# One core, attention and two feed-forward layers: the first batch's rows of values for local attention issued on ScalarE's DMA queue

## The chip, the core and the metric

The kernel runs on one core of a Trainium2 chip. Five engines work side by side, each with its own list of instructions that it takes strictly in order: PE (TensorE, matmuls and transposes on the tensor engine), DVE (VectorE), ACT (ScalarE), POOL (GpSimd) and SP (SyncE, which here only issues transfers). A transfer (DMA) is issued by an engine's instruction and then moved by 16 DMA engines. Engines wait for one another, and for transfers, through semaphores. The metric is the time of one execution on the device in microseconds (us); lower is better.

## The reference

Three layers follow one another. B = 4 batches, H = 8 heads, S = 576 positions, D = 64.

```python
# attention: a downsampled branch plus a local branch
q_d, k_d, v_d = means of q, k, v over groups of 4 positions
out_d = softmax(scale * q_d @ k_d^T) @ v_d          # repeated 4 times along S
scores = where(|i - j| < 4, scale * q @ k^T, -1e9)  # local: 7 diagonals
out_local = softmax(scores) @ v
x = (out_up + out_local) as [2304, 512]
# first feed-forward layer: [512 -> 2048 -> 512], ELU between
x = elu(x @ moe_w_in) @ moe_w_out
# second: gated, [512 -> 1536 -> 512]
out = (silu(x @ moe2_w_gate) * (x @ moe2_w_val)) @ moe2_w_out
```

The weights come as 64-bit floats and are unpacked into 32-bit ones on the chip.

## The kernel before

**Units.** Local attention of one batch is cut into six *units* of 96 positions. A unit loads its rows of q (192 KB), of k (224 KB) and of v (256 KB; four pieces of 32 rows, or five where a piece at the sequence's edge is split). In the code these are `load_rows`, called from `add_unit` and, for v, from the inner function `load_values`. PE transposes q and k (L495), ACT or DVE copies the transposed rows out of PSUM (L276 or L278, `qT` and `kT`), sums over groups of four go into `sums` (L506, L508, L509), PE computes the scores (L524), DVE masks them (L536) and takes maxima (L541), ACT takes exponentials (L548), the weights are transposed (L559) and spread (`bd`), and PE multiplies with v (L578); the result is copied to `f`.

**The downsampled branch.** When all six units' q and k are in `sums`, four pairs of heads follow (`add_pooled`): scores on PE (L619), maxima on DVE (L626), exponentials on ACT (L632, four per pair), normalizing on DVE (L638, L639, L642), transposes on PE (L660), products on PE (L673), copied into `xdT`. Their values are eight loads of 144 KB (L607).

**The feed-forward layers.** `x` is `f` plus `xdT` (L693). The work is cut into chunks of three units (288 positions). Chunk 0 of the first layer uses whole 32-bit products (L740 and L745, here called gemm1 and gemm2, 16 steps of 128 hidden columns each); later chunks split each number into two parts and make three products (L715 to L717). 32 weight tiles of 512 KB are loaded in the order in, out, in, out (L332, L337), 14 of them into places that are free from the start; ACT and DVE unpack them (L374, L377, L381, L383).

**Order.** All work is put into tasks by `add(engine, cost, due, fn, ...)`: each has an engine, an estimated cost and a due time, and a small event loop (`Work.run`) starts on each engine the ready task that is due first. The order that this gives is the order of each engine's instructions. The first batch's v rows were tasks of SP with cost 2.0 and a due time of their own (`v_due`), between q, k and the weights.

**Completion counters.** Every transfer signals its landing on one of eight counters, shown as DMAHW0 to DMAHW7 in the built program, which are handed out in turn. A transfer that takes a counter waits, on the engine that issues it, until the transfer that had the counter before has landed. When all transfers are issued by SP, each waits for the one eight places ahead of it.

Of the kernel before, what the change touches and what calls it, by code (L numbers as in the profile page):

```python
# [19 lines left out]
P = 128  # L20
R = 4
W = 2 * R - 1
QB = 32
# [7 lines left out]
UPC = 3  # L31
# [26 lines left out]
class Half(Buf):  # L58
# [5 lines left out]
    t = property(lambda self: False if self.whole.t is None else self.whole.t[:, self.i])  # L64
# [164 lines left out]
def attention_moe_moe(ctx: ExitStack, tc: tile.TileContext, q, k, v, w_in, w_out, w_gate, w_val, w_o2, ident_in, mask_in, band_in, picks_in, out):  # L229
    nc = tc.nc  # L230
    B, H, S, D = q.shape
# [40 lines left out]
    COPIER = "act", "dve"  # L272
# [13 lines left out]
    add = work.add  # L286
# [167 lines left out]

        return source[name][b, h0:h1].rearrange("h (u p r) d -> u p h (r d)", u=2, r=R)[u]

    def load_rows(name, b, first, count, t, p0=0):

        nc.sync.dma_start(  # L459
            out=t[p0:p0 + count].rearrange("p (h d) -> p h d", d=D),  # L460
            in_=source[name][b, :, first:first + count].rearrange("h t d -> t h d"))

    sums = {}

    def add_unit(n, due, load_due, rows=None, after=(), then=(), late=0.0, v_due=None, first=None):

        b, i = divmod(n, NU)
        q0 = i * U
        k0 = min(max(q0 - 8, 0), S - KU)
        off = PAD + q0 - k0  # L470
        tq, tk, tv = rows if rows else (qk_rows.new(), qk_rows.new(), v_rows.new())
        add("sp", 0.5, load_due, lambda: load_rows("q", b, q0, U, tq.t), writes=[tq], nbytes=U * H * D * 4 * 1.9, after=after)
        add("sp", 0.5, load_due + 0.1, lambda: load_rows("k", b, k0, KU, tk.t), writes=[tk], nbytes=KU * H * D * 4 * 1.9, after=after)

        def load_values():
            for s in range(NB):
                first = q0 + s * SB - (R - 1)
                lo, hi = max(first, 0), min(first + QB, S)
                p0 = s * QB + lo - first
                if hi - lo < QB:  # L480
                    nc.gpsimd.memset(tv.t[s * QB:(s + 1) * QB], 0.0)

                for a in range(lo, hi, QB // 2 if hi - lo < QB else QB):
                    load_rows("v", b, a, min(hi - a, QB // 2 if hi - lo < QB else QB), tv.t, p0 + a - lo)

        add("sp", 2.0, load_due + 4.0 if v_due is None else v_due, load_values, writes=[tv], nbytes=P * H * D * 4 * 3.1, after=after)
        if i == 0:
            sums[b] = sum_ring.new()
        qT, kT = place("qT"), place("kT")
        for which, t, dst, count, start, own in ((0, tq, qT, U, 0, 0), (1, tk, kT, KU, PAD, off)):  # L490
            pt = att_bank()

            def turn(t=t, count=count, pt=pt):
                for p in range(NP):
                    nc.tensor.transpose(pt.t[:, p * count:(p + 1) * count], t.t[:count, p * P:(p + 1) * P], ident[:count, :count])  # L495

            def keep(engine, dst=dst, count=count, start=start, pt=pt):
                copy(engine, dst.t[:, :, start:start + count], pt.t[:, :NP * count].rearrange("p (a t) -> p a t", a=NP))

            half = half_ring.new()  # L500

            def pool(engine, which=which, dst=dst, own=own, half=half):
                x = dst.t[:, :, own:own + U].rearrange("p a (g r) -> p a g r", r=R)
                to = sums[b].t[:, which, :, i * GU:(i + 1) * GU]
                if engine == "dve":
                    nc.vector.tensor_reduce(out=to, in_=x, op=ALU.add, axis=X)  # L506
                else:
                    nc.gpsimd.tensor_tensor(out=half.t, in0=x[:, :, :, :2], in1=x[:, :, :, 2:], op=ALU.add)  # L508
                    nc.gpsimd.tensor_tensor(out=to, in0=half.t[:, :, :, 0], in1=half.t[:, :, :, 1], op=ALU.add)  # L509

            begin = due if first is None else first
            add("pe", 0.4, begin - EAGER, turn, reads=[t], writes=[pt, dst], slack=SLACK, after=then)
            add(COPIER, (0.5, 0.55), begin + 1, keep, reads=[pt], writes=[dst], second=1)
            add(EITHER, (0.56, 1.1), begin + 2, pool, reads=[dst], writes=[sums[b], half])

        sc = [att_bank(), att_bank()]
        due += late

        def scores():
            for p in range(NP):  # L520
                for s in range(NB):
                    first = off + s * SB - (R - 1)
                    for j in range(2):
                        nc.tensor.matmul(  # L524
                            sc[j].t[s * QB:(s + 1) * QB, p * QB:(p + 1) * QB],
                            qT.t[j * D:(j + 1) * D, p, s * SB:s * SB + QB], kT.t[j * D:(j + 1) * D, p, first:first + QB],
                            start=True, stop=True)

        sm, st, pt, bd, pv = small["sm"].new(), small["st"].new(), small["pt"].new(), place("bd"), att_bank()

        add("pe", 0.8, due + 2 - EAGER, scores, reads=[qT, kT], writes=[*sc, sm], slack=SLACK)
        edge = 0 if i == 0 else 2 if i == NU - 1 else 1

        def masked():
            for j in range(2):
                nc.vector.tensor_tensor(  # L536
                    out=sm.t[:, j * NP:(j + 1) * NP], in0=sc[j].t[:, :NP * QB].rearrange("p (a k) -> p a k", a=NP),
                    in1=mask[:, edge:edge + 1].to_broadcast([P, NP, QB]), op=ALU.add)

        def maxima():  # L540
            nc.vector.reduce_max(out=st.t.rearrange("p h o -> p (h o)"), in_=sm.t, axis=X)  # L541

        def less(engine):
            two(engine).tensor_tensor(out=sm.t, in0=sm.t, in1=st.t.to_broadcast([P, H, QB]), op=ALU.subtract)

        def exps():
            x = sm.t.rearrange("p h k -> p (h k)")
            nc.scalar.activation(x, x, AF.Exp, scale=scale)  # L548

        def total():  # L550
            nc.vector.reduce_sum(out=st.t.rearrange("p h o -> p (h o)"), in_=sm.t, axis=X)
            nc.vector.tensor_scalar_add(st.t, st.t, 1e-9)
            nc.vector.reciprocal(out=st.t, in_=st.t)

        def weight(engine):
            two(engine).tensor_tensor(out=sm.t, in0=sm.t, in1=st.t.to_broadcast([P, H, QB]), op=ALU.mult)

        def turn_weights():
            nc.vector.transpose(out=pt.t.rearrange("p h k -> p (h k)"), in_=sm.t.rearrange("p h k -> p (h k)"))  # L559

        def spread(engine):
            for s in range(NB):
                rows = slice(s * QB, (s + 1) * QB)
                copy(engine, bd.t[rows, :, s * SB:(s + 1) * SB], pt.t[rows, :, :SB])

        add("dve", 0.56, due + 3, masked, reads=sc, writes=[sm])
        add("dve", 0.42, due + 3.1, maxima, reads=[sm], writes=[st])
        add(EITHER, (0.62, 0.65), due + 3.2, less, reads=[sm, st], writes=[sm])
        add("act", 0.4, due + 4, exps, reads=[sm], writes=[sm])
        add("dve", 0.8, due + 4.5, total, reads=[sm, st], writes=[st])  # L570
        add(EITHER, (0.5, 0.65), due + 5, weight, reads=[sm, st], writes=[sm])
        add("dve", 0.42, due + 5.5, turn_weights, reads=[sm], writes=[pt])
        add(("act", "dve"), (1.4, 1.5), due + 6, spread, reads=[pt], writes=[bd], second=1)

        def values():
            for p in range(NP):
                for j in range(2):
                    nc.tensor.matmul(  # L578
                        pv.t[j * D:(j + 1) * D, p * U:(p + 1) * U], tv.t[:, (2 * p + j) * D:(2 * p + j + 1) * D],
                        bd.t[:, j * NP + p], start=True, stop=True)  # L580

        xf = xf_ring.new()
        add("pe", 0.7, due + 7 - EAGER, values, reads=[tv, bd], writes=[pv, xf], slack=SLACK)
        add(COPIER, (0.5, 0.55), due + 8, lambda engine: copy(engine, xf.t, pv.t[:, :NP * U]), reads=[pv], writes=[xf], second=1)
        return xf
# [298 lines left out]
    with tc.manual_schedule():  # L884
# [9 lines left out]
        rows = [parts(2) for _ in range(NU)]  # L894
        vals = [x for _ in range(NU // 2) for x in parts(2)]
# [25 lines left out]

        xfs = {}
        for n in range(NU):
            xfs[n] = add_unit(n, 4.0 * n, -40 + 2 * n, rows=(*rows[n], vals[n]), late=0.0 if n < UPC else 24.0,
                v_due=-20.0 + n if n < UPC else 30.0 + n, first=0.5 * n - 8.0)
            if n == 0:
                load_mask()
        for p in range(NP):
# [6 lines left out]
        kept = {}  # L935
# [91 lines left out]
```

## Time and profile before

| | |
|---|---|
| median of 3 runs | 1028.29 us (1024.51 to 1029.45) |
| profiled execution | 1029.34 us, of which 1027.2 us span from first to last instruction |
| PE busy | 994.0 us, 97% of the span |
| DVE, ACT, POOL busy | 516.5, 414.5, 311.6 us |
| mean granted TensorE clock | 0.975 |
| moved by DMA | 91.19 MB |

Busy time is the time in which an engine executes. A wait shows as idle time in front of an instruction, with the name of what ended it. Because the engines take their lists in order, an instruction that waits holds back everything behind it on its engine.

### The profile page before, as it was taken

The page shows a single profiled execution, that of the slowest core. Times are in us where ns is not written, and L with a number is a line of the kernel's source. Part 1 is how long each engine was busy: PE and PEld are TensorE (multiplying, and loading weights), DVE is VectorE, ACT ScalarE, POOL GpSimd, SP SyncE. Part 2 cuts the span into 40 slices and gives each one's busy share as a digit, 9 for nine tenths or more (in the row PEclk, how much of TensorE's full clock was granted, in tenths as well). Part 3 has the DMA queues.
Part 4 walks back from the last instruction along what each step waited for, and adds up shares of the span by engine and source line. Part 5 has one row for each costly group of instructions (what it writes and reads, how often), then busy time and mean ns, then how long its engine had stood idle before and what let it go on. Part 6 is the DMA issues. An engine that isn't in the chain of part 4 may idle for free.

```text
span 1027.2 us, 19351 instructions
## 1 busy us (share of the span) xinstructions
PE 994.0 (97%) x7540; PEld 868.7 (85%) x7540; DVE 516.5 (50%) x1063; ACT 414.5 (40%) x1015; POOL 311.6 (30%) x358
## 2 busy tenths in 40 slices
PE   5899999899999999998999999999999999999998
PEld 4667789899998999998999888888888888888897
DVE  5888888876778767884124422232223222322232
ACT  4688865465554555545345421121112111211111
POOL 5230993652337333356259710010001000000000
PEclk8599999999999999999999999999999999999999
DMA  9799333654545654436024420020002000100000
GB/s 165 231 314 246 70 89 107 156 149 128 135 119 123 157 156 118 116 82 204 1 84 136 126 61 0 1 83 1 1 1 72 0 1 11 41 1 1 11 32 21
DMA packets 129003, 91.19 MB, mean 89 GB/s; under 512 B 73744, under 2 KB 116880, under 8 KB 128912
## 3 DMA queue, kind: packets, MB, share of 16 engines
q1 hardware_dynamic: 128768, 89.70, 32.4%
q8 instruction: 59, 0.97, 0.4%
q14 instruction: 32, 0.26, 0.1%
q10 hardware_dynamic: 144, 0.26, 0.1%
HBM read 71.06 MB, written 18.87 MB: 88 GB/s over the span
## 4 chain that ended last, share of the span: by engine, by line
PE 84%; DVE 7%; DMA 4%; SPq 2%; issue 2%; ACT 1%; POOL 0%; DVEq 0%; ACTq 0%; POOLq 0%
PE bank L715 25%; PE bank L716 24%; PE bank L717 24%; PE bank L740 2%; PE bank L745 2%; PE bank L578 1%; SPq L459 1%; DMA rows<-in_q_dram 1%; PE bank L524 1%; PE bank L495 1%; DVE mid L353 1%; PE bank L619 1%; DMA w<-in_moe_w_in_dram 1%; DVE f L693 1%; DMA w<-in_v_dram 1%
## 5 line engine op out<-in xcount | busy, mean ns | idle before, releaser
L715 PE MATMUL bank<-x,w 128*128 128x288 f32 (+2 forms) x928 | 318.0, 343 | 3.1 <-DVE e L788 2.6
L716 PE MATMUL bank<-x,w 128*128 128x288 f32 (+2 forms) x928 | 313.0, 337 | 0.0
L717 PE MATMUL bank<-x,w 128*128 128x288 f32 (+2 forms) x928 | 311.8, 336 | 0.0
L861 DVE TENSOR_TENSOR e<-bank,e 128x512 f32<-128x512 f32 (+1 forms) x120 | 76.3, 637 | 260.9 <-ACT e L858 179.3
L715 PEld LDWEIGHTS bank<-x,w 128*128 128x128 f32 x928 | 176.2, 190 | 25.0 <-DVE e L788 4.3
L716 PEld LDWEIGHTS bank<-x,w 128*128 128x128 f32 x928 | 176.7, 190 | 16.9 <-POOL x L703 0.3
L717 PEld LDWEIGHTS bank<-x,w 128*128 128x128 f32 x928 | 176.6, 190 | 16.8
L795 POOL TENSOR_TENSOR g<-e,g 128x288 fp32r<-128x288 f32 x112 | 94.9, 848 | 169.5 <-ACT g L276 124.9
L715 PE MATMUL bank<-g,w 128*128 128x288 f32 x448 | 135.2, 302 | 2.0 <-ACT o L276 2.0
L716 PE MATMUL bank<-g,w 128*128 128x288 f32 x448 | 132.3, 295 | 0.0
L717 PE MATMUL bank<-g,w 128*128 128x288 f32 x448 | 132.0, 295 | 0.0
L858 ACT ACTIVATE e<-bank 128x512 f32<-128x512 f32 (+1 forms) x60 | 33.2, 555 | 188.3 <-PE bank L717 188.3
L838 POOL TENSOR_TENSOR x<-x2r,x 128x512 fp32r<-128x512 f32 (+1 forms) x20 | 23.5, 1194 | 269.7 <-ACT x L837 269.7
L863 ACT CAST y<-e 128x512 fp32r<-128x512 f32 (+1 forms) x60 | 34.6, 577 | 156.3 <-DVE e L861 134.4
L715 PEld LDWEIGHTS bank<-g,w 128*128 128x128 f32 x448 | 84.4, 188 | 4.7 <-ACT o L276 2.3
L788 DVE SCALAR_TENSOR_TENSOR e<-e,bank 128x288 f32<-128x288 f32 x112 | 49.9, 446 | 72.8 <-ACT e L792 66.8
L716 PE MATMUL bank<-w,y 128*128 128x512 f32 x216 | 85.7, 397 | 0.0
L715 PE MATMUL bank<-w,y 128*128 128x512 f32 x216 | 85.3, 395 | 0.0
L716 PEld LDWEIGHTS bank<-g,w 128*128 128x128 f32 x448 | 84.9, 189 | 0.2
L717 PE MATMUL bank<-w,y 128*128 128x512 f32 x216 | 84.9, 393 | 0.0
L717 PEld LDWEIGHTS bank<-g,w 128*128 128x128 f32 x448 | 84.6, 189 | 0.0
L784 ACT ACTIVATE e<-bank 128x288 f32<-128x288 f32 x112 | 45.9, 410 | 84.8 <-PE bank L717 58.1
(118 smaller groups left out, 1399.1 us busy)
## 6 DMA issues: line engine op xcount, KB each, us to landing
wd<-mid SPq DMA_DIRECT2D x72, 128.0 KB
u<-wd SPq DMA_DIRECT2D x36, 256.0 KB
w<-in_moe_w_in_dram SPq DMA_DIRECT2D x16, 512.0 KB
w<-in_moe_w_out_dram SPq DMA_DIRECT2D x16, 512.0 KB
w<-in_moe_w_gate_dram SPq DMA_DIRECT2D x24, 256.0 KB
w<-in_moe_w_val_dram SPq DMA_DIRECT2D x24, 256.0 KB
w<-in_moe_w_out_dram SPq DMA_DIRECT2D x24, 256.0 KB
out_dram<-x2r SPq DMA_DIRECT2D x17, 256.0 KB
```

The source lines that it names most:

```text
L715: nc.tensor.matmul(ps, sh, mh, start=first, stop=False)
L716: nc.tensor.matmul(ps, sh, ml, start=False, stop=False)
L717: nc.tensor.matmul(ps, sl, mh, start=False, stop=last)
L740: nc.tensor.matmul(h.t[:, :T1], wi.t[:, i * P:(i + 1) * P].bitcast(F32), x.t[:, i, 0].bitcast(F32), start=i == 0, stop=i == NP - 1)
L745: nc.tensor.matmul(acc[0][i].t[:, :T1], wo.t[:, i * P:(i + 1) * P].bitcast(F32), ge(), start=f == 0, stop=f == NF1 - 1)
L784: nc.scalar.activation(e.t, h.t[:, :T1], AF.Relu, scale=-1.0)
L788: nc.vector.scalar_tensor_tensor(out=e.t, in0=e.t, scalar=-1.0, op0=ALU.add, in1=h.t[:, :T1], op1=ALU.max)
L795: add("pool", 0.82, due - URGENT, lambda e=e, g=g: nc.gpsimd.tensor_tensor(out=g.t[:, 1], in0=e.t, in1=g.t[:, 0], op=ALU.subtract), reads= ...
L838: add("pool", 1.3, due, lambda T=T, raw=raw, x=x: nc.gpsimd.tensor_tensor(out=x.t[:, 1, :T], in0=raw.t[:, :T], in1=x.t[:, 0, :T], op=ALU.s ...
L858: add("act", 0.6, due, lambda T=T, e=e, gate=gate: nc.scalar.activation(e.t[:, :T], gate.t[:, :T], AF.Sigmoid), reads=[gate], writes=[e], ...
L861: add("dve", 0.64, due, lambda T=T, e=e, x=x: nc.vector.tensor_tensor(out=e.t[:, :T], in0=x.t[:, :T], in1=e.t[:, :T], op=ALU.mult), reads= ...
L863: add("act", 0.6, due, lambda T=T, e=e, y=y: nc.scalar.copy(y.t[:, 0, :T], e.t[:, :T]), reads=[e], writes=[y])
```

## The change

For the first batch (`b == 0`) the v rows of all six units are issued by ACT (`nc.scalar.dma_start`) instead of SP. The task is an ACT task with cost 0.4 and a due time of -50, so it goes out as soon as it is ready. For units 0 to 2 it is ready when that unit's q has been copied out of PSUM, and that copy is now always ACT's. For units 3 to 5 it is ready when the unit before has taken its exponentials. The other batches are as before.

```diff
-    def load_rows(name, b, first, count, t, p0=0):
-
-        nc.sync.dma_start(
+    def load_rows(name, b, first, count, t, p0=0, queue=None):
+
+        (queue or nc.sync).dma_start(
...
-                    load_rows("v", b, a, min(hi - a, QB // 2 if hi - lo < QB else QB), tv.t, p0 + a - lo)
-
-        add("sp", 2.0, load_due + 4.0 if v_due is None else v_due, load_values, writes=[tv], nbytes=P * H * D * 4 * 3.1, after=after)
+                    load_rows("v", b, a, min(hi - a, QB // 2 if hi - lo < QB else QB), tv.t, p0 + a - lo,
+                        None if b else nc.scalar)
+
+        if b:
+            add("sp", 2.0, load_due + 4.0, load_values, writes=[tv], nbytes=P * H * D * 4 * 3.1, after=after)
...
-            add(COPIER, (0.5, 0.55), begin + 1, keep, reads=[pt], writes=[dst], second=1)
+            kept = add(*((COPIER, (0.5, 0.55)) if b or which else ("act", 0.5)), begin + 1, keep if b or which else lambda keep=keep: keep("act"),
+                reads=[pt], writes=[dst], second=1)
+            if not b and not which and n < UPC:
+
+                add("act", 0.4, -50.0, load_values, writes=[tv], nbytes=P * H * D * 4 * 1.9, after=[kept])
...
-        add("act", 0.4, due + 4, exps, reads=[sm], writes=[sm])
+        shown[n] = add("act", 0.4, due + 4, exps, reads=[sm], writes=[sm])
...
+        if not b and n >= UPC:
+            add("act", 0.4, -50.0, load_values, writes=[tv], nbytes=P * H * D * 4 * 1.9, after=[shown[n - 1]])
```

Three places show how the order moves. The first is ACT early in the program, at the copy of unit 2's q and the first exponentials (`sm`). Before:

```order
L276 COPY kT<-bank 128x4x112 [waits PE_49,Pool_49]
L276 COPY qT<-bank 128x4x96 [waits DVE_49,PE_49]
L548 ACTIVATE sm<-sm 128x256 [waits DVE_49]
L276 COPY kT<-bank 128x4x112 [waits PE_49,Activation_49]
L276 COPY qT<-bank 128x4x96 [waits PE_49,Activation_49]
```

Now, at the same place (`w<-in_v_dram` are loads of v rows; PE_49, DVE_49 and the like are the engines' own semaphores):

```order
L276 COPY kT<-bank 128x4x112 [waits PE_49]
L276 COPY qT<-bank 128x4x96 [waits DVE_49,PE_49]
L459 DMA w<-in_v_dram 32x8x64 [waits DMAHW6_49]
L459 DMA w<-in_v_dram 32x8x64 [waits DMAHW0_49]
L459 DMA w<-in_v_dram 32x8x64 [waits DMAHW3_49]
L459 DMA w<-in_v_dram 32x8x64 [waits DMAHW6_49]
L554 ACTIVATE sm<-sm 128x256 [waits DVE_49]
L276 COPY kT<-bank 128x4x112 [waits PE_49,Activation_49]
```

Unit 2's four loads now stand between the copy and the exponentials, each with a wait for a counter; the first two counters belong to unit 5's q and k, the third to the second of the eight loads of pooled values, the fourth to the first load of this group itself. Five loads of unit 0 and four of unit 1 stand likewise behind the two earlier copies of q.

The second place is ACT just ahead of the first exponentials of the downsampled branch (`w,su`). Before:

```order
L276 COPY kT<-bank 128x4x112 [waits PE_49,Activation_49]
L548 ACTIVATE sm<-sm 128x256 [waits Activation_49,Pool_49]
L276 COPY f<-bank 128x384 [waits PE_49] x2
L632 ACTIVATE w,su<-bank,nm 72x144 [waits DVE_49]
L632 ACTIVATE w,su<-bank,nm 72x144 x3
```

Now, from the third of unit 4's four loads on (`L374` and `L377` unpack weights):

```order
L459 DMA w<-in_v_dram 32x8x64 [waits DMAHW4_49]
L459 DMA w<-in_v_dram 32x8x64 [waits DMAHW5_49]
L554 ACTIVATE sm<-sm 128x256 [waits DVE_49,Activation_49]
L374 ACTIVATE bank<-w 128x512
L459 DMA w<-in_v_dram 32x8x64 [waits DMAHW6_49]
L459 DMA w<-in_v_dram 32x8x64 [waits DMAHW7_49]
L459 DMA w<-in_v_dram 32x8x64 [waits DMAHW0_49]
L459 DMA w<-in_v_dram 16x8x64 [waits DMAHW1_49,Pool_49]
L459 DMA w<-in_v_dram 11x8x64 [waits DMAHW2_49]
L377 ACTIVATE w<-w 128x512
L641 ACTIVATE w,su<-bank,nm 72x144 [waits DVE_49,PE_49]
```

The downsampled branch's exponentials (now L641) stand behind the loads of units 3, 4 and 5. Unit 3's four loads stand further up on the same engine, behind the exponentials of unit 2; they wait for DMAHW4, 6, 0 and 2, which belong to the last load of pooled values, to unit 2's last load, and to the third and the fifth weight.

The third place is SP at the weights. Before, the loads of units 3 to 5 stand behind the ninth weight:

```order
L332 DMA w<-in_moe_w_in_dram 128x4x256 [waits DMAHW4_49]
L337 DMA w<-in_moe_w_out_dram 128x1024 [waits DMAHW5_49]
L332 DMA w<-in_moe_w_in_dram 128x4x256 [waits DMAHW6_49]
L459 DMA w<-in_v_dram 32x8x64 [waits DMAHW7_49]
L459 DMA w<-in_v_dram 32x8x64 [waits DMAHW0_49]
```

Now all 14 weights that have a place follow the pooled values without a break; these are the tenth to the fourteenth, and the first load of pooled values of the next batch (`praw`) behind them:

```order
L337 DMA w<-in_moe_w_out_dram 128x1024 [waits DMAHW3_49]
L332 DMA w<-in_moe_w_in_dram 128x4x256 [waits DMAHW4_49]
L337 DMA w<-in_moe_w_out_dram 128x1024 [waits DMAHW5_49]
L332 DMA w<-in_moe_w_in_dram 128x4x256 [waits DMAHW6_49]
L337 DMA w<-in_moe_w_out_dram 128x1024 [waits DMAHW7_49]
L616 DMA praw<-in_v_dram 72x2x256 [waits DMAHW1_49]
```

A transfer signals on the counter that it waits for, and both queues draw on the same eight. So ACT's waits for DMAHW4, 5, 6 and 7 at the second place are waits for the eleventh, twelfth, thirteenth and fourteenth weight, and its wait for DMAHW1 is one for the `praw` load.

## Rows read from the trace of the kernel before

**Rows 1.** The page, part 1: busy us (share of the span) and instructions.

```profile
PE 994.0 (97%) x7540; PEld 868.7 (85%) x7540; DVE 516.5 (50%) x1063; ACT 414.5 (40%) x1015; POOL 311.6 (30%) x358
```

**Rows 2.** Windows by stage: busy us (instructions), clock, DMA share, GB/s.

```profile
0.00:51.95 51.95, 36.85 (x620) 27.96 (x620) 35.86 (x97) 28.11 (x85) 19.87 (x42) 0.67 0.85 197
51.95:132.00 80.05, 77.33 (x584) 59.69 (x589) 66.89 (x125) 67.48 (x142) 38.44 (x39) 0.98 0.74 204
...
160.00:1027.00 867.00, 852.83 (x5960) 756.06 (x5958) 388.27 (x786) 302.40 (x743) 230.03 (x254) 0.99 0.26 72
```

**Rows 3.** Timeline of PE: start, us, work [idle before, releaser].

```profile
25.83 1.55 PE L578 MATMUL bank<-bd,w 128*64 128x96 f32 x16 [1.41 <-DMA w<-in_v_dram]
27.30 2.20 PE L619 MATMUL bank<-sums 64*72 64x144 f32 x16
...
48.05 2.83 PE L578 MATMUL bank<-bd,w 128*64 128x96 f32 x32
51.95 5.92 PE L740 MATMUL bank<-x,w 128*128 128x288 f32 x16 [1.08 <-ACT f L276]
57.80 0.88 PE L578 MATMUL bank<-bd,w 128*64 128x96 f32 x16
...
66.49 2.21 PE L740 MATMUL bank<-x,w 128*128 128x288 f32 x8 [1.70 <-DVE w L383]
...
96.59 0.52 PE L495 MATMUL bank<-ident,rows 96*128 96x96 f32 x4 [0.71 <-DMA rows<-in_q_dram]
```

**Rows 4.** Timeline of SP's queue, the loads of v.

```profile
13.61 5.87 SPq L607 DMA_DIRECT2D w<-in_v_dram  x8
20.02 8.74 SPq L459 DMA_DIRECT2D w<-in_v_dram  x13
...
34.41 16.28 SPq L459 DMA_DIRECT2D w<-in_v_dram  x13
```

**Rows 5.** Chain that ended last, in order of time: start, us, what.

```profile
14.85 5.76 DMA w<-in_v_dram
...
22.82 2.87 DMA w<-in_v_dram
```

**Rows 6.** Waits of SP's queue, 30 to 52 us: total, times, longest.

```profile
SPq L459 <- DMA w<-in_moe_w_in_dram: 2.7, 2, 2.0
SPq L459 <- DMA w<-in_moe_w_out_dram: 0.9, 1, 0.9
```

**Rows 7.** Instructions of L459: duration in ns, min/median/max.

```profile
L459 SPq DMA_DIRECT2D w<-in_v_dram x26: 311/450/2467, 20.0 to 50.3; - x26
```

**Rows 8.** Timeline of ACT.

```profile
8.11 0.48 ACT L276 COPY qT<-bank 128x384 f32<-128x384 f32 x1
9.34 0.53 ACT L276 COPY kT<-bank 128x448 f32<-128x448 f32 x1 [0.75 <-PE bank L495]
...
12.26 0.42 ACT L548 ACTIVATE sm<-sm 128x256 f32<-128x256 f32 x1
...
31.40 0.38 ACT L632 ACTIVATE w<-bank,nm 72x144 f32<-72x144 f32 x1
```

**Rows 9.** Windows, columns as in rows 2.

```profile
4.00:17.00 13.00, 7.85 (x217) 5.36 (x214) 5.95 (x17) 6.84 (x14) 4.38 (x12) 1.00 1.30 203
17.00:20.00 3.00, 2.60 (x89) 2.21 (x90) 2.16 (x8) 0.95 (x3) 0.85 (x2) 0.67 0.80 199
31.00:42.00 11.00, 7.82 (x118) 6.04 (x120) 8.89 (x28) 8.55 (x39) 1.90 (x2) 0.50 1.05 377
...
34.42:49.60 15.18, 12.57 (x156) 10.25 (x158) 13.59 (x37) 11.10 (x37) 4.68 (x7) 0.50 0.92 270
...
8.11:31.40 23.29, 15.73 (x412) 12.89 (x412) 17.67 (x52) 10.39 (x25) 10.38 (x20) 0.71 0.92 171
```

**Rows 10.** Timeline of DVE: the downsampled branch's first normalizing, and chunk 0's input.

```profile
34.42 0.15 DVE L638 TENSOR_SCALAR su<-su 72x4 f32<-72x4 f32 x1
...
49.59 2.17 DVE L693 TENSOR_TENSOR x<-f,xdT 128x384 f32<-128x384 f32 x3
```

More of the change, by code (lines that the diff above doesn't have):

```diff
@@ L455, in rows_of, with add_unit @@
         return source[name][b, h0:h1].rearrange("h (u p r) d -> u p h (r d)", u=2, r=R)[u]
-    def load_rows(name, b, first, count, t, p0=0):
-        nc.sync.dma_start(
+    def load_rows(name, b, first, count, t, p0=0, queue=None):
+        (queue or nc.sync).dma_start(
             out=t[p0:p0 + count].rearrange("p (h d) -> p h d", d=D),
             in_=source[name][b, :, first:first + count].rearrange("h t d -> t h d"))
-    sums = {}
-    def add_unit(n, due, load_due, rows=None, after=(), then=(), late=0.0, v_due=None, first=None):
+    sums, shown = {}, {}
+    def add_unit(n, due, load_due, rows=None, after=(), then=(), late=0.0, first=None):
         b, i = divmod(n, NU)
@@ L923, in attention_moe_moe @@
         for n in range(NU):
-            xfs[n] = add_unit(n, 4.0 * n, -40 + 2 * n, rows=(*rows[n], vals[n]), late=0.0 if n < UPC else 24.0,
-                v_due=-20.0 + n if n < UPC else 30.0 + n, first=0.5 * n - 8.0)
+            xfs[n] = add_unit(n, 4.0 * n, -40 + 2 * n, rows=(*rows[n], vals[n]), late=0.0 if n < UPC else 24.0, first=0.5 * n - 8.0)
             if n == 0:
```

## The prediction

> **What bounds the kernel now.** I read the page's first part, then the windows by stage, then the chain of waits and the engines' timelines at the start. PE is busy 97% of the span [rows 1]. The windows show where the other 3% lie: from 51.95 us on, PE is busy in all but a few per cent of every stretch, while in the first 51.95 us it is busy 36.85 us at a mean granted clock of 0.67 [rows 2]. 51.95 us is the start of gemm1, the first product of the feed-forward layers [rows 3]. The end is therefore that start plus about 975 us of products, and a change in the prologue is worth what it does to that start and to the few waits behind it.
>
> The prologue runs on transfers and then on a chain of small steps. SP issues q and k, the pooled values, 13 v loads, nine weights and 13 more v loads; the two groups of v loads hold SP for 8.74 and 16.28 us [rows 4]. PE waits 1.41 us for unit 0's v at 25.83 us and only then begins the downsampled branch's scores at 27.30 us [rows 3]. That branch's first exponential starts at 31.40 us [rows 8] and gemm1 follows 20.55 us later. Why SP needs 16.28 us for 13 loads of 64 KB: a transfer waits where it is issued until the one that had its counter before has landed. The trace shows this: the v loads behind nine weights wait for weights to land, 2.7 and 0.9 us in two rows [rows 6], and the chain runs from the second load of pooled values, issued at 14.85 us and landed 5.76 us later, to SP's v loads [rows 5].
>
> **The change, part by part.** *SP.* It sheds 26 issues, 25.0 us of its time [rows 4]. The first weight can go out right behind the pooled values instead of at 28.8 us, and 14 follow without a break. What that can save on PE is bounded by waits that late v rows or weights cause now: 1.41 us at 25.83, up to 1.55 us of unit 0's product that stands ahead of the downsampled scores, 1.70 us for an unpacked weight at 66.49 and 0.71 us for rows of batch 1 at 96.59 [rows 3]: 5.4 us at most.
>
> The Trainium skill, DMA: Bandwidth & Descriptors, section "Issuing engines are not separate DMA queues", says that transfers of all issuers run on the same 16 engines and that a second issuer saves only the sequencer's issue time, usually small. By that rule alone the change is worth between nothing and those 5.4 us. The rows put the saved time at 25.0 us of SP, so "usually small" does not hold here.
>
> *ACT.* It gains 26 issues. A v load takes 0.45 us at the median, 0.31 to 2.47 [rows 7]: 11.7 us, 8 to 64 at the ends. ACT is busy 10.39 of the 23.29 us up to 31.40 [rows 9], so the median would nearly fit into idle time. What does not fit are the waits: an issue on ACT that waits for a counter holds every copy and exponential behind it, on which PE, DVE and POOL wait.
>
> The same page, section "Anatomy of one DMA", says that a semaphore wait happens on the issuing sequencer before dispatch. Rows 6 agree (2.7 us on SP); no row of before shows it on ACT.
>
> I follow ACT through its list. For volumes I use the rates of the windows: 203 GB/s for rows of 256 bytes, 199 for pooled values, 377 for weights, from 4.0 us on [rows 9].
>
> 1. Units 0 and 1. The five loads stand behind the first copy, which ends at 8.59 us [rows 8]. The fifth waits for the first (issued by 9.05 us) to land; a small load lands 2.87 us after its issue [rows 5], so it goes at about 11.8 and the copy of kT at 12.2 instead of 9.34 [rows 8]. Unit 1's fourth load waits in turn for that fifth: 11.8 + 2.87 = 14.7 us, the copy behind it at 15.1.
> 2. Unit 2. Its first two loads wait for unit 5's q and k. Ahead of these lie 64 + 16 + 6 x 416 = 2576 KB on SP and 506 KB on ACT, 3.16 MB: 4.0 + 15.5 = 19.5 us. The third waits for a load of pooled values, the fourth for the first (near 18.7 + 2.87): about 22 us. Unit 0's exponentials, at 12.26 now [rows 8], come at 22; the copies for units 3 to 5 stand behind them. PE and DVE run out of work meanwhile.
> 3. Unit 3. Its last two loads wait for the third and fifth weight. Pooled values end at 26.7 us (below), five weights take 2.62 MB / 377 = 7.0: about 34 us.
> 4. Units 4 and 5. They wait for weights 11 to 14 and for a load behind the fourteenth. Volume up to there: 2576 KB plus 762 KB of v at 203 (16.8 us), 1152 KB of pooled values at 199 (5.9 us): 26.7 us; 14 x 512 KB at 377 (19.5 us) and six v loads among them, 384 KB at 203 (1.9 us): 48.1 us. Four issues of 0.45 and one unpacking of some 0.5 us follow. The downsampled branch's first exponential starts at 50.4 us instead of 31.40: 19.0 later.
>
> The ends for step 4: all 12.3 MB at 377 from 4.0 us, with the same 2.3 us behind them, gives 39.0 (7.6 later); unit 5's issues at 2.47 us each give about 61 (30 later). I take 50.4, since the windows hold exactly these kinds of transfer.
>
> 5. From that exponential to gemm1. Now 20.55 us: 3.02 us until DVE's first normalizing at 34.42, then 15.18 us up to 49.60 of which DVE is busy 13.59, then 2.17 for the input [rows 9, 10]. In the new order DVE can begin after four exponentials (1.4 us) and has what else it had done already: 1.4 + 13.59 + 2.17 = 17.2 us. The end on the other side is 20.55. I take 17.2: gemm1 at 67.6 us, 15.65 later.
> 6. Behind it. The wait of 1.70 us for a weight goes, since the weights are long there. Units 3 and 4's products, 2.83 us ahead of gemm1 now, stand behind it; at 0.88 us a unit [rows 3] they cost 1.8 there. I set both against each other, 0 us (ends: -2.4 and +1.8). All else on PE keeps its length.
>
> Sum: 1029.34 + 15.65 = 1045.0 us in the terms of the profiled execution, which lies 1.05 us above the median of 1028.29: **1044.0 us**, 1.5% more.
>
> **The rivals.** *Faster.* Counters come free in time, ACT's issues hide in its idle 12.9 us [rows 9], and PE sheds its waits: 1028.3 - 5.4 = 1022.9 us. For it speaks SP's 25.0 us; against it that unit 2's loads cannot go before unit 5's k has landed, which the volume puts past 17 us even without any v ahead of it. It decides if the first exponential still starts by 31.4 us.
>
> The Trainium skill, Perfetto Trace Analysis, section "DMA Optimizations", says that where descriptor generation is the bottleneck, balancing transfers over the engines that can issue may help. This is that rival; the DMA share of 1.05 between 31 and 42 us [rows 9] speaks for engines that move data rather than wait for issues.
>
> *No change.* ACT is held, but the lost time comes back: the 1.70 and 0.71 us waits go, DVE takes copies from ACT, and the DMA engines reach 377 GB/s for small rows too. Then the first exponential is some 7.6 us late (the low end of step 4), step 5 gives back 3.35 and the later waits 2.4: +1.9, 1030.2 us. The rate of 203 at a DMA share of 1.30 [rows 9] speaks against it.
>
> *Much slower.* Step 5 saves nothing: 1028.3 + 19.0 = 1047.3; with each of unit 5's issues 0.5 us longer, 1050.
>
> **How the numbers follow.** A difference within 0.5% (5.1 us) is about what a measurement of this kernel can tell from no change. The forecast, with the much slower case in it, gets 0.80: both counters and volumes force ACT's waits, and only their length is open. No change gets 0.12, faster 0.08. The forecast's own range is 1036 to 1051 us (step 4 between 8 us earlier than taken and the last rival), and holds most, some 0.70 of all. To reach 8 in 10 it is led down into no change: 1028 to 1051. Faster by over 0.5% 0.08, within 0.12, slower 0.80.
>
> **What would show it.** In the profile after, ACT's queue should hold 26 issues of L459, with unit 0's exponentials near 22 us, unit 3's last v load near 34, unit 5's second near 48, the downsampled branch's first exponential near 50 and gemm1 near 68; the stretch behind gemm1 should be as long as now within 3 us. SP should have issued 14 weights by about 45 us. Wrong would be the volumes if weights land much earlier than 48 us, the order of waits if ACT's idle time before its loads names no transfers, and step 5 if gemm1 follows the first exponential by 20 us or more. If gemm1 starts by 54 us, the whole forecast falls.

## The result

The changed kernel takes 1038.15 us (median of 4 runs, 1037.54 to 1040.1) against 1027.3 us of before in the same comparison: a ratio of 1.0114, 95% interval 1.0094 to 1.0134. That is slower, inside the forecast range and 5.9 us below the forecast. The profiled execution took 1040.1 us. Lines behind the change are shifted by two to nine: local scores are L530, their exponentials L554, the products with v L587, the downsampled branch's exponentials L641, gemm1 L749, the three products L724 to L726.

The page of the changed kernel, part 1, against [rows 1], and the issues of v on ACT's queue (duration in ns, min/median/max), against [rows 7], where all 26 were SP's:

```profile
PE 988.2 (95%) x7540; PEld 863.5 (83%) x7540; DVE 511.5 (49%) x1071; ACT 412.4 (40%) x1007; POOL 309.4 (30%) x357
...
L459 ACTq DMA_DIRECT2D w<-in_v_dram x26: 317/318/639, 6.9 to 55.3; - x26
```

Its timeline of ACT, against [rows 8]:

```profile
6.76 1.28 ACT L276 ACT_TABLE_LOAD   x1 [6.76 <-PE bank L497]
6.89 1.45 ACTq L459 DMA_DIRECT2D w<-in_v_dram  x3
8.06 0.48 ACT L276 COPY qT<-bank 128x384 f32<-128x384 f32 x1
...
11.62 0.54 ACT L276 COPY kT<-bank 128x448 f32<-128x448 f32 x1 [3.09 <-DMA w<-in_v_dram]
...
16.63 0.54 ACT L276 COPY kT<-bank 128x448 f32<-128x448 f32 x1 [4.09 <-DMA w<-in_v_dram]
...
26.05 0.42 ACT L554 ACTIVATE sm<-sm 128x256 f32<-128x256 f32 x1 [8.51 <-DMA w<-in_v_dram]
...
37.33 0.48 ACT L276 COPY f<-bank 128x384 f32<-128x384 f32 x1 [5.03 <-DMA w<-in_moe_w_in_dram]
...
50.28 0.42 ACT L554 ACTIVATE sm<-sm 128x256 f32<-128x256 f32 x1 [6.13 <-DMA w<-in_v_dram]
...
55.72 0.66 ACT L377 ACTIVATE w<-w 128x512 int32<-128x512 uint32 x1 [4.51 <-DMA w<-in_v_dram]
56.29 0.36 ACT L641 ACTIVATE w<-bank,nm 72x144 f32<-72x144 f32 x1
```

Each bracket is ACT's idle time ahead of the row. Up to 66 us six waits of ACT name transfers; they stand in four rows and make 31.3 us in all (us, times, longest):

```profile
ACT sm L554 <- DMA w<-in_v_dram: 14.6, 2, 8.5
ACT kT L276 <- DMA w<-in_v_dram: 7.2, 2, 4.1
...
ACT f L276 <- DMA w<-in_moe_w_in_dram: 5.0, 1, 5.0
ACT w L377 <- DMA w<-in_v_dram: 4.5, 1, 4.5
```

The chain of the changed kernel that ended last (start, us, what), against [rows 5]: from 8.76 us on it runs through two loads of v on ACT, a load of pooled values that SP issues at 20.70, and three weights; the last of them is issued at 42.45 and landed at 53.92, and 2.37 us later the downsampled branch begins. In the built program all these transfers have one counter, DMAHW7 (unit 0's fourth load, unit 1's third, the fifth load of pooled values, weights 2, 8 and 14, then unit 5's second load), so that each, on whichever engine, went out only when the one before it had landed.

```profile
8.76 5.37 DMA w<-in_v_dram
14.15 6.53 DMA w<-in_v_dram
20.70 5.54 DMA w<-in_v_dram
26.25 5.54 DMA w<-in_moe_w_out_dram
31.80 10.63 DMA w<-in_moe_w_out_dram
42.45 11.45 DMA w<-in_moe_w_out_dram
53.92 1.82 DMA w<-in_v_dram
...
56.29 1.54 ACT w L641 x8
...
74.29 4.18 PE bank L749 x8
```

gemm1 starts at 74.29 instead of 51.95 us [rows 3], 22.3 us later, while the span grew by only 11.1 (1027.2 to 1038.3). Windows of the changed kernel (columns as in [rows 2]) say where the rest is: chunk 0 from gemm1 to the first of the three products takes 69.11 us, 68.84 before (51.95 to 120.79); what follows takes 894.90 us, 906.4 before (120.79 to 1027.2). The first two rows are the kernel before, the others the changed one:

```profile
51.95:120.79 68.84, 66.12 (x412) 50.62 (x412) 57.05 (x103) 57.67 (x119) 28.61 (x31) 0.97 0.80 223
120.79:1027.20 906.41, 891.02 (x6508) 790.17 (x6508) 423.59 (x865) 328.77 (x813) 263.08 (x286) 0.99 0.26 72
...
25.30:53.92 28.62, 12.13 (x272) 10.11 (x272) 16.69 (x49) 10.38 (x26) 11.21 (x21) 0.62 0.98 300
...
74.29:143.40 69.11, 68.57 (x443) 52.52 (x444) 61.34 (x110) 58.15 (x119) 35.38 (x36) 0.96 0.60 171
143.40:1038.30 894.90, 884.34 (x6512) 784.25 (x6510) 415.02 (x869) 323.96 (x801) 254.34 (x280) 1.00 0.27 73
```

So two questions stand: is it ACT's waiting that makes gemm1 late, and what gave 11 us back far behind it?

### The profile page after: what moved, and what is told of

Its sections match the earlier page's. It is cut to its first block, busy times and chain, and to the rows that moved or that the text cites. A ratio compares the mean times of both kernels' runs of the same rounds, so it can differ in the third digit from the quotient of the medians.

```text
span 1038.3 us, 19355 instructions
## 1 busy us (share of the span) xinstructions
PE 988.2 (95%) x7540; PEld 863.5 (83%) x7540; DVE 511.5 (49%) x1071; ACT 412.4 (40%) x1007; POOL 309.4 (30%) x357
## 4 chain that ended last, share of the span: by engine, by line
PE 87%; DMA 6%; DVE 4%; ACT 1%; issue 1%; SPq 0%; POOL 0%; DVEq 0%; ACTq 0%; POOLq 0%
PE bank L724 26%; PE bank L725 25%; PE bank L726 25%; PE bank L749 3%; PE bank L754 3%; DMA w<-in_moe_w_out_dram 3%; DMA w<-in_v_dram 2%; PE bank L587 1%; PE bank L530 1%; PE bank L497 1%; PE bank L669 1%; PE bank L682 1%; PE bank L628 1%; DMA wd<-mid 1%; DVE f L702 1%
## 5 line engine op out<-in xcount | busy, mean ns | idle before, releaser
L724 PE MATMUL bank<-x,w 128*128 128x288 f32 (+2 forms) x928 | 315.9, 340 | 4.0 <-DVE e L797 3.8
L726 PE MATMUL bank<-x,w 128*128 128x288 f32 (+2 forms) x928 | 309.9, 334 | 0.0
L724 PEld LDWEIGHTS bank<-x,w 128*128 128x128 f32 x928 | 174.3, 188 | 26.2 <-DVE e L797 5.6
L725 PEld LDWEIGHTS bank<-x,w 128*128 128x128 f32 x928 | 174.9, 188 | 18.2 <-POOL x L712 1.6
L726 PEld LDWEIGHTS bank<-x,w 128*128 128x128 f32 x928 | 174.7, 188 | 16.8
L804 POOL TENSOR_TENSOR g<-e,g 128x288 fp32r<-128x288 f32 x112 | 92.3, 824 | 149.1 <-ACT g L276 101.4
L724 PE MATMUL bank<-g,w 128*128 128x288 f32 x448 | 135.1, 302 | 0.0
L726 PE MATMUL bank<-g,w 128*128 128x288 f32 x448 | 131.9, 294 | 0.0
L724 PEld LDWEIGHTS bank<-g,w 128*128 128x128 f32 x448 | 84.1, 188 | 2.2 <-issue 1.2
L724 PE MATMUL bank<-w,y 128*128 128x512 f32 x216 | 85.3, 395 | 0.0
L726 PE MATMUL bank<-w,y 128*128 128x512 f32 x216 | 84.9, 393 | 0.0
L726 PEld LDWEIGHTS bank<-g,w 128*128 128x128 f32 x448 | 84.5, 189 | 0.0
```

Source lines behind the costliest of these rows:

```text
L724: nc.tensor.matmul(ps, sh, mh, start=first, stop=False)
L725: nc.tensor.matmul(ps, sh, ml, start=False, stop=False)
L726: nc.tensor.matmul(ps, sl, mh, start=False, stop=last)
L804: add("pool", 0.82, due - URGENT, lambda e=e, g=g: nc.gpsimd.tensor_tensor(out=g.t[:, 1], in0=e.t, in1=g.t[:, 0], op=ALU.subtract), reads= ...
```

## The experiments

**Theory:** ACT waits, as issuer, for transfers, and everything behind it is late. **Rivals:** the order of work that the change brings costs or gains by itself; issuing as such costs; SP, not ACT, is late; lateness at the start gives itself back. "Against before" is the difference of the medians in one comparison.

| kernel | time, us | against before, us | ratio, 95% interval |
|---|---|---|---|
| old order, loads on SP, again | 1026.7 (one run) | -0.2 | |
| new order, loads on SP | 1019.91 | -7.0 | 0.9932 (0.9919 to 0.9944) |
| old order, loads on ACT | 1052.98 | +26.0 | 1.0256 (1.0238 to 1.0274) |
| old order, PE delayed | 1044.86 | +17.9 | 1.0168 (1.0153 to 1.0182) |
| new order, units 0 to 2 on ACT | 1025.38 | -1.4 | 0.9985 (0.9969 to 1.0) |
| new order, units 3 to 5 on ACT | 1028.02 | +1.3 | 1.0012 (0.9998 to 1.0025) |
| new order on SP, ACT held 43.7 us | 1051.69 | +26.4 | 1.0252 (1.0236 to 1.0268) |
| new order on SP, ACT held 31.1 us | 1037.95 | +11.2 | 1.0114 (1.0097 to 1.0131) |
| old order, planned with 0.16 | 1029.72 | +3.0 | 1.0028 (1.0009 to 1.0047) |
| old order, planned with 0.14 | 1021.52 | -3.8 | 0.9961 (0.9947 to 0.9976) |
| new order on SP, planned with 0.16 | 1031.07 | +5.8 | 1.004 (1.0025 to 1.0055) |
| new order on SP, planned with 0.14 | 1028.41 | +3.1 | 1.0026 (1.0014 to 1.0039) |

### Order and queue taken apart

The kernel before once more, for the scatter of its profile:

> The kernel before, unchanged, for a second profile. The first one lost time behind gemm1 to idle PE and to a lower clock (window from 120.79 us on: 906 us, against 895 us for the same work after the change). If these losses belong to the order of the work, they stand at the same places again and the stretch from the first three-product matmul to the end is 904 to 908 us. If they come by chance in one execution, the stretch is several us shorter or longer.

```profile
121.67:1024.60 902.93, 886.16 (x6508) 785.63 (x6508) 423.31 (x865) 329.53 (x813) 263.29 (x286) 1.00 0.26 73
```

The stretch is 3.5 us shorter than in the first profile, just outside the range for losses that belong to the order. The two parts of the loss differ: PE's idle time is there again (902.93 - 886.16 = 16.8 us, 15.4 in the first profile), while the time lost to a lower clock is not (PE busy 886.16 us at 1.00, 891.02 at 0.99). A difference of some 3.5 us in this stretch is therefore within what two executions of one kernel show.

The changed kernel with its order, but all loads on SP's queue:

```diff
-                        None if b else nc.scalar)
+                        None)
```

> The order of all compute work is that of the changed kernel, to the instruction; only the 26 v loads are issued on SP at their place in the program. Theory: ACT's waits for counters made gemm1 late, so gemm1 starts again near 52 us (47 to 57). Rival 1, the new order of the prologue made it late: gemm1 at 66 us or later, time near 1038. Where the 11 us went that came back behind gemm1: if the new order of batches 1 to 3 is better by itself, the time is 1027 - 11 = 1016 us; if they came back because gemm1 was late, 1025 to 1029 us.

The kernel before with its order, but the loads of the first batch's v on ACT's queue:

```diff
-                    load_rows("v", b, a, min(hi - a, QB // 2 if hi - lo < QB else QB), tv.t, p0 + a - lo)
+                    load_rows("v", b, a, min(hi - a, QB // 2 if hi - lo < QB else QB), tv.t, p0 + a - lo, None if b else nc.scalar)
```

> The order of all compute work is that of the kernel before, to the instruction; only the 26 v loads are issued on ACT at their place in the program. Theory: ACT waits for counters, with unit 5's loads in front of the downsampled branch's first exponential again, behind fewer weights; gemm1 12 to 24 us later than 52. If the new order gave the 11 us back, nothing comes back here: 1039 to 1051 us. If lateness gave them back: 1030 to 1040 us.

The new order on SP is faster than both kernels, 1019.91 us, with gemm1 at 51.91 as the theory said; the time lies between the two that were expected, since chunk 0 takes 72.74 us in this order, 68.84 in the kernel before. The old order on ACT takes 2 us more than the upper end of what was expected, with gemm1 at 80.72 us, 28.8 later. The queue alone costs 26.0 us in the old order and 17.9 in the new one (from -7.0 to the changed kernel's +10.9). In the old order ACT's waits name transfers as well, 32.9 us of them up to 66 us; why nearly the same wait costs 8 us more there was not tested.

```profile
ACT sm L548 <- DMA w<-in_v_dram: 14.5, 1, 14.5
...
ACT kT L276 <- DMA w<-in_v_dram: 6.7, 1, 6.7
ACT qT L276 <- DMA w<-in_v_dram: 6.4, 2, 4.8
ACT sm L548 <- DMA w<-in_moe_w_out_dram: 5.3, 1, 5.3
```

The Trainium skill, DMA: Bandwidth & Descriptors, section "Issuing engines are not separate DMA queues", says that a second issuer saves only the time that a sequencer takes to issue. At one order the runs show that it can also cost: the same loads on a second issuer are 17.9 and 26.0 us dearer.

In the chain of the new order on SP, the exponentials that started at 56.29 and gemm1 that started at 74.29 are 22 us earlier:

```profile
34.50 1.54 ACT w L641 x8
...
51.91 4.18 PE bank L749 x8
```

Its windows from 24.73, gemm1 and the first three products on:

```profile
24.73:46.00 21.27, 15.26 (x243) 12.37 (x242) 16.68 (x50) 15.13 (x55) 6.35 (x12) 0.66 1.01 308
...
51.91:124.65 72.74, 69.08 (x445) 52.02 (x445) 61.66 (x110) 58.68 (x120) 36.39 (x37) 0.97 0.67 180
124.65:1018.10 893.45, 884.34 (x6511) 784.20 (x6509) 417.57 (x869) 324.79 (x800) 254.31 (x280) 1.00 0.27 74
```

The last stretch takes 893.45 us here, where nothing is late, and 894.90 in the changed kernel. The old order takes 902.93 us there when it is on time (the run of before again), and still 904.68 with its loads on ACT (gemm1 at 80.72 us). What came back there, 8 to 11.5 us by which profile of before it is measured, belongs to the order, not to the lateness.

The waits of PE between 150 and 600 us show a part of it. They add up to 10.1 and 11.6 us in the two profiles of before, to 6.4 in the changed kernel and 4.8 in the new order on SP. Three waits stand in both profiles of before and in neither of the new order: 2.2 us for a `qT` that DVE copies (L495), 2.1 us for scores that DVE masks (L578, waiting for L536) and 2.0 us for a copy `o` of ACT (L715).

### Does a late start give itself back?

The kernel before with the first product of gemm1 repeated; the output is kept, the work of PE grows.

```diff
-            for i in range(NP):
+            for i in [i for _ in range(1 if f else 12) for i in range(NP)]:
```

> The kernel before with the first gemm1 step (4 matmuls, 1.94 us at full clock) made 12 times instead of once: everything behind it is 22 to 25 us later, nothing else changes, the result is the same. If lateness of PE against loads and the other engines gives 11 us back: 1036 to 1041 us. If only the new order does: 1048 to 1052 us.

The first products of gemm1 take 27.31 us (x104) instead of 5.92 (x16) [rows 3], 21.4 more, and the time grows by 17.9, between the two ranges that were expected. Some 3.5 us come back, inside chunk 0 (it takes 87.36 us, 66.0 without the added work, against 68.84 and 70.43 in the two profiles of before), and nothing behind it: 903.92 us from the first three products on, against 902.93 and 906.4 undelayed. In the new order it is alike: chunk 0 takes 72.74 us with the loads on SP and 69.11 in the changed kernel, 3.6 less.

### Half of the loads

Units 0 to 2 on ACT, then units 3 to 5 on ACT, the others on SP, both in the new order:

```diff
-                        None if b else nc.scalar)
+                        nc.scalar if not b and n < UPC else None)
...
-                        None if b else nc.scalar)
+                        nc.scalar if not b and n >= UPC else None)
```

> Only the 13 loads of v of units 0 to 2 stay on ScalarE's queue; those of units 3 to 5 go back to SyncE's, in the new order of work. Theory (the time lost is ScalarE's waiting for transfers that its counters belong to): ACT still waits for unit 5's q and k and for a load of pooled values, so unit 0's exponentials start near 22 to 26 us, but no wait of ACT is for a weight; the downsampled branch's first exponential is near 40 to 45, gemm1 near 58 to 62, the total 1025 to 1031. Rival 1 (only waits for weights cost anything; the early ones are caught up): gemm1 within 2 us of 51.9, total 1018 to 1022. Rival 2 (ScalarE loses a fixed time for each load that it issues): half of the 18.2 us, total 1029, and the companion with units 3 to 5 gives the same.

Units 0 to 2 cost 5.7 us (from -7.0 to -1.4). The first exponentials are at 26.58 us, L641 at 42.64 and gemm1 at 62.55, as the theory said but for half a microsecond at the first and the last. Three waits of ACT name transfers, all of them loads of v, and make 15.4 us (7.7 in two before `kT`, 7.7 in one before `sm`); none names a weight, so the early waits are not caught up, against rival 1.

> Only the 13 loads of v of units 3 to 5 stay on ScalarE's queue; those of units 0 to 2 go back to SyncE's, in the new order of work. The counters fall otherwise than in the changed kernel: ACT's loads now wait for unit loads of q and v, two loads of pooled values, the second weight and ACT's own earlier loads, and for no later weight. Theory (what costs is whose landing ACT waits for): ACT's waits for transfers add up to under 10 us instead of 31.3, the downsampled branch's first exponential is near 35 to 40, gemm1 near 52 to 56, the total 1019 to 1024, though ACT issues the very loads that in the changed kernel stood behind the weights. Rival (it is the issuing itself, or the place behind the exponentials, that costs): half of the 18.2 us or more, total 1029 to 1036, gemm1 at 60 to 70.

Here the theory's sum was right and its conclusion wrong: ACT waits 7.9 us for loads of v and 2.0 for a weight that it unpacks, yet L641 starts at 45.50 (expected 35 to 40), gemm1 at 63.51 (expected 52 to 56, 60 to 70 by the rival), and it costs 8.3 us. SP's queue, two pairs of rows from the chain that ended last, and ACT's timeline show what was missing:

```profile
13.25 8.12 SPq L459 DMA_DIRECT2D w<-in_v_dram  x5
```

```profile
19.07 1.97 DMA w<-in_v_dram
21.05 0.31 SPq L459
...
38.17 6.16 DMA w<-in_v_dram
44.35 0.53 ACTq L459
```

```profile
25.27 0.48 ACT L276 COPY f<-bank 128x384 f32<-128x384 f32 x1 [5.64 <-PE bank L587]
...
37.37 0.42 ACT L554 ACTIVATE sm<-sm 128x256 f32<-128x256 f32 x1 [1.32 <-DMA w<-in_v_dram]
...
44.93 0.66 ACT L377 ACTIVATE w<-w 128x512 int32<-128x512 uint32 x1 [6.63 <-DMA w<-in_v_dram]
```

The coupling goes both ways. In the built program the fifth load of unit 0's v, on SP, has the counter of the first load that ACT issues, which stands behind exponentials and goes out at 19.07 us; SP's five loads therefore last until 21.37 (in the run on SP they took 3.53 us, from 14.52 on), and the copy of the product `f` starts at 25.27 instead of 22.41. On ACT, unit 5's fifth load waits 6.63 us for unit 5's first, which it had just issued. These two and the wait of 1.32 us ahead of the exponentials at 37.37 make 2.9 + 1.3 + 6.6 = 10.8 of the 11.0 us by which L641 is late. So the rival, a cost of the issuing itself, is not needed here; the next section takes the issues off ACT altogether.

### ACT held by something else

All loads on SP, in the new order; at the six places of the loads ACT takes short exponentials of a tile of its own, which compute nothing of the output (second run: 7, 9, 19, 11, 14, 10).

```diff
+    held = [10, 13, 26, 16, 19, 14]
...
-                        None if b else nc.scalar)
+                        None)
+            if not b:
+                for _ in range(held[n]):
+                    nc.scalar.activation(idle, idle, AF.Exp, scale=-1.0)
```

> All loads on SyncE in the new order, as in the version that measured 1019.9 us; at the six places where the changed kernel has ACT's loads of v, ACT takes 98 short exponentials of a tile of its own instead (10, 13, 26, 16, 19 and 14 of them, some 0.32 us each), about as long in all as the 31.3 us that ACT waited for transfers. What is added computes nothing of the output. Theory (ACT being held is enough, whatever holds it): the downsampled branch's first exponential at 46 to 54 us instead of 34.5, gemm1 at 62 to 72 instead of 51.9, total 1029 to 1037. Rival (what costs is on SyncE, whose weights and pooled values wait in turn for loads that ACT issues late): gemm1 by 56, total at most 1023.

> As the run in which ACT was held by short exponentials of a tile of its own and all loads stayed on SyncE, but 70 of them (7, 9, 19, 11, 14, 10), since one took 0.446 us there instead of 0.32: 31.2 us in all, as long as the changed kernel's ACT waited for transfers. If ACT being held explains the loss: by proportion from that run the downsampled branch's first exponential at 56 to 60 us, gemm1 at 73 to 77 and the total at 1038 to 1046, as in the changed kernel (56.29, 74.29, 1038.15) or a few us above it. If SyncE's part (weights landing late) matters as much: gemm1 by 68 and the total at most 1033.

The first run missed in size: one took 0.446 us from start to start, so ACT was held 43.7 us, and it gave 1051.69 us, 33.4 above the order on SP. The second held it 31.1 us (timeline of ACT, then the window from the first three products on; the held rows are L490 here, and lines behind them lie five further on):

```profile
9.34 3.10 ACT L490 ACTIVATE idle<-idle 128x256 bf16<-128x256 bf16 x7
...
13.13 4.01 ACT L490 ACTIVATE idle<-idle 128x256 bf16<-128x256 bf16 x9
...
17.83 8.49 ACT L490 ACTIVATE idle<-idle 128x256 bf16<-128x256 bf16 x19
...
32.27 4.88 ACT L490 ACTIVATE idle<-idle 128x256 bf16<-128x256 bf16 x11
...
43.42 6.22 ACT L490 ACTIVATE idle<-idle 128x256 bf16<-128x256 bf16 x14
...
50.40 4.43 ACT L490 ACTIVATE idle<-idle 128x256 bf16<-128x256 bf16 x10
...
55.28 0.36 ACT L646 ACTIVATE w<-bank,nm 72x144 f32<-72x144 f32 x1
```

```profile
142.47:1036.10 893.63, 884.76 (x6511) 784.34 (x6509) 413.00 (x869) 323.25 (x800) 254.69 (x280) 1.00 0.27 74
```

The downsampled branch at 55.28, gemm1 at 73.30, 1037.95 us in all: the changed kernel's 56.29, 74.29 and 1038.15, with no load on ACT. SP, which waited for no load of ACT's, issued the fourteenth weight at 40.60 us (41.24 in the run on SP, 42.45 in the changed kernel), and that was no help. Holding ACT for as long as it waited for transfers reproduces the whole loss. The cost against the order on SP is 18.2 us for 31.1 of hold and 33.4 for 43.7: what does not show in the time, 12.9 and 10.3 us, is a remainder, and 12.6 us more of hold cost 15.2 more.

### Is the new order's gain its own?

Old and new order, all loads on SP, each planned with a latency between engines of 0.16 and of 0.14 instead of 0.15:

```diff
-    LATENCY = 0.15
+    LATENCY = 0.16
```

> The kernel before with one number of the planner changed (its assumed latency between engines 0.16 instead of 0.15), which moves hundreds of instructions and nothing that is meant to matter; all loads on SyncE. If the 7 us that the new order gave by itself with all loads on SyncE is the luck of an order, this one scatters as far: 1017 to 1037, off 1027 by 4 us or more. If orders of this kernel agree closely and the gain belongs to the change's order: 1025 to 1029.

> The new order with all loads on SyncE (1019.9 us), planned with an assumed latency of 0.16 instead of 0.15, which moves many instructions. If the 7 us of the new order belong to the change's tasks: 1016 to 1023. If they are the luck of one order: 1023 to 1034, as the old order with 0.16 gave 1029.7.

> The kernel before, planned with a latency of 0.14 instead of 0.15. If orders of the kernel before lie close together: 1025 to 1031, with the products behind the first three-product taking 902 to 907 us. Luck of the order: outside of that, down to 1015.

> The new order with all loads on SyncE, planned with a latency of 0.14. Gain of the change's tasks: 1016 to 1023. Luck of one order: 1023 to 1034.

A number that means nothing for the chip moves the old order from -3.8 to +3.0 us and the new one from -7.0 to +5.8. Three of the four came out as said for the luck of an order; the old order with 0.16 lies between its two ranges. Over the three plans the means are -0.3 and +0.6, while single plans of one order lie 7 and 13 us apart. So the 7 us belong to one plan, and a gain of the change's tasks as such does not show; one of a few us could hide in this scatter. A further plan of the old order, with another assumed fixed time of a transfer (2.2 instead of 2.0), deadlocks and has no time. One window each, from the first three products to the end, of the old order planned with 0.16 and with 0.14:

```profile
122.11:1028.70 906.59, 887.87 (x6508) 785.88 (x6508) 424.83 (x871) 330.37 (x817) 252.82 (x274) 1.00 0.26 72
...
119.26:1019.50 900.24, 886.79 (x6508) 786.04 (x6508) 415.71 (x846) 335.99 (x838) 258.74 (x275) 1.00 0.26 73
```

PE sits idle 18.7 and 13.5 us there, against 9.1 in the new order on SP. The new order itself takes 903.74 and 901.32 us in this stretch when it is planned with 0.16 and 0.14, instead of 893.45.

## Why the prediction was right, and where it was not

Direction and mechanism hold: ACT waits where it issues, and what stands behind it is late. The Trainium skill, DMA: Bandwidth & Descriptors, section "Anatomy of one DMA — SWDGE (gpsimd) path", says that any semaphore wait happens on the issuing sequencer before dispatch. The changed kernel now shows it on ACT's queue too, with 31.3 us. The sizes, by the prediction's steps:

1. Units 0 and 1: the copies at 11.62 and 16.63 us, forecast 12.2 and 15.1. Held within 1.5 us.
2. Unit 2: exponentials at 26.05, forecast 22. The time for a small load to land was mis-sized: 2.87 us was taken, and the chain shows 5.37 and 6.53 for loads of v among the others (and 5.54 for a load of pooled values).
3. Unit 3: the copy behind its last load at 37.33, forecast about 34; about as late as unit 2 was.
4. Units 4 and 5: the fourteenth weight landed at 53.92, forecast 48.1, and the first exponential came at 56.29, forecast 50.4. The 2.3 us between them held (2.37). The error was in the stretch of the weights, mostly in its rate: the forecast had 7.73 MB in 21.4 us from 26.7 on (weights at 377, rows at 203 GB/s), 361 GB/s in all; the window from 25.30 to 53.92 shows 300 at a DMA share of 0.98, which is 8.6 MB in 28.62 us. At 361 these 8.6 MB would take 23.8 us, so that about 4.8 us are the rate and 2.4 the larger volume, in which are the two `praw` loads from 44.17 us on; 1.4 us of earlier start stand against them. The 377 had been read for weights alone, but the window it comes from, 31 to 42 us, holds loads of v as well, from 34.41 us on [rows 4]. The run on SP has 308 at 1.01 in its window, so the mixture moves at much the same rate whoever issues. Why it is no faster was not tested.
5. From there to gemm1: 18.0 us, forecast 17.2. Held; but all of it starts 5.9 later, so that gemm1 is 22.3 us late instead of 15.65.
6. Behind gemm1: forecast 0 with ends of -2.4 and +1.8, measured -11.2 (+0.3 in chunk 0, -11.5 behind it), and -9.4 against the second profile of before. This is the step that failed, and with it the sign that was set for it, a stretch as long as now within 3 us. "All else on PE keeps its length" took the order behind chunk 0 for unchanged, and the diff's tasks re-planned it too: with the loads back on SP the new order keeps 893.45 us behind chunk 0.

The sum: 15.65 + 6.65 - 11.2 = 11.1 us, the growth of the span. The forecast of +15.65 was close by luck, because two errors of 6.7 and 11.2 us offset each other.

Of the rivals, *faster* named an idle time of ACT of 12.9 us in which issues would hide; the waits were 31.3, and SP's 25.0 us were worth nothing: in the new order the first and the fourteenth weight go out at 24.73 and 41.24 us with all loads on SP, and at 25.30 and 42.45 without them. *No change* needed the lost time to come back in later waits; a delay by itself gives back 3.5 us. *Much slower* is close to what gemm1 did, +22.3.

Left open: how a plan comes to its waits of PE behind chunk 0, 9 to 19 us in all; the runs name some of these waits, not why one order has them and another not.

## What to carry to other kernels

A transfer moved to a compute engine's queue takes its wait along: list, for each issue, which earlier transfer has its completion counter, and ask when that one lands. Here everything behind the issue on ACT waited with it, and the old queue came to wait for loads of the new one too. Before a difference below one per cent is put down to a change that re-plans the program, undo the change inside the new plan, and vary a number of the planner that should not matter, to see what the plan alone does. Here moving the loads back inside the new plan is the best version found, 1019.91 us, but that gain is a plan's luck.

## What the runs showed that was not expected

An issue on ACT did not wait for ACT's work ahead of it: three loads that stand behind the first copy went out at 6.89 us, while ACT loaded its table (6.76 to 8.04) and before that copy began at 8.06. And the issues themselves cost almost nothing that shows: an issue held ACT's queue for 0.318 us at the median, at 11.67 us one ran beside a copy (11.62 to 12.16), and a hold of 31.1 us with no issue on ACT took the same time as 31.3 us of waits with 26 of them. So the 11.7 us that the prediction took for the issues were no cost of their own; the cost was the waiting.
